# The last weight row and its copy loaded first, each in 16 pieces, and three more filler matmuls ahead of the weight matmuls

## The chip, the cores and the metric

The kernel runs on one core of one Trainium2 chip. The metric is device time in microseconds (us) of one launch; less is better. The engines are named as in the profile: PE is TensorE's matmuls and PEld its weight loads, DVE is VectorE, ACT is ScalarE, POOL is GpSimd, and SP is SyncE, which here does nothing but issue DMAs. An engine name with a q (SPq) is that engine's instruction queue.

## The reference

A circular two-dimensional convolution of one image of 224 x 224 pixels and 96 channels with 7 x 7 weights of 96 x 96, computed with FFTs, in bfloat16 at both ends:

```python
# x: (1, 224, 224, 96)   w: (7, 7, 96, 96)
wp = jnp.pad(w, ((0, H - K), (0, W - K), (0, 0), (0, 0)))
Xf = rfft2(x.astype(float32), axes=(1, 2))
Wf = rfft2(wp.astype(float32), axes=(0, 1))
Yf = einsum('bhwi,hwio->bhwo', Xf, Wf)
y = irfft2(Yf, s=(H, W), axes=(1, 2)).astype(bfloat16)
```

## The kernel before

**How the work is cut.** Along the image's rows the kernel transforms, along its columns it convolves directly. The 224 rows are cut into 8 blocks of 28 rows with 6 rows of overlap, so a block is a signal of length 34, with 17 frequencies of a real and an imaginary part. The 224 columns are cut into 7 tiles of 32 pixels. For each tile, stage A transforms the rows by matmuls of pixels against the matrix `Fm` and puts the result into `xf`; stage B convolves along the columns, frequency by frequency, with the transformed weights `WF` (`b_round`, one call for a frequency), using sums and differences of `xf` that DVE puts into `J`; stage C transforms back by matmuls against `G` and writes the rows out. Between B and C the data passes through a scratch tensor in device memory (`scr`, then `tt`).

**The weights.** The 49 weight matrices (7 x 7 places) are loaded into the tile `wqx`, two partitions for each place k: partition 2k holds the 96 x 96 matrix as one run, and partition 2k + 1 holds the same run shifted by 48 output channels. `PW` is 49, `C` is 96, `C2` is 48, and `WC` is the length of a run, 96 x 96 - 48 = 9168 elements or 18336 bytes. The part of the tile from column `WC` on holds a small matrix `Em`, computed on the chip by DVE, and zeros. One matmul of the loaded weights (the stationary side, with a step of 96 elements from column to column) against `Em` gives the transformed weights of two output channels. `prep_jobs(gi)` makes these matmuls for the frequencies of group gi, four matmuls to a PSUM bank, and `evac` has DVE or ACT copy each bank into `WF`. Every such matmul reads all 98 partitions of `wqx`, so the first one needs every weight DMA to have landed, the last row's too. The page calls the tile wq.

**The order of the DMAs.** All loads of the opening are issued by SP in the program's order (the wrapper `_Ordered` fixes the order of each engine's instructions and of all transfers): first the six wrapped pixels of each half of the block rows (`xh_bufs`), then the 32 pixels of tile 0's first half, `load_x(0, 0)`, then the weights, then tile 0's second half, `load_x(0, 1)`. A pixel load is two DMAs, one of 112 rows and one of 6. The weights are two DMAs as well, one of the first 48 places (96 partitions) and one of the last place (2 partitions):

```python
for k, n in ((0, PW - 1), (PW - 1, 1)):
    dma(wqx[2 * k:2 * (k + n), 0:WC], bass.AP(wsrc.tensor, wsrc.offset + k * C * C, [[C * C, n], [C2, 2], [1, WC]]))
```

The buffers of tile 0's pixels lie in a part of `WF` that is filled late, so the profile shows these loads as WF<-in_x_dram.

**The order of PE's work in the opening.** PE starts with filler matmuls (`warm(n)`: n matmuls of 512 columns on zeros, whose results nobody reads), 17 of them. Stage A of the wrapped pixels and of tile 0's first half follows, then the lines around the second edit:

```python
for _ in range(3):
    warm(9)
for f in prep_jobs(0)[0]:
    f()
last = [f() for f in fj[0][1]]
```

That is 27 fillers, then the 48 matmuls that transform the weights of the first two frequencies (`prep_jobs(0)`), then stage A of tile 0's second half for frequencies 0 to 7 (`fj[0][1]`: 32 matmuls in four banks), whose first copy is also what the loads of tile 1's pixels wait for. After that DVE builds the first `J`, stage B begins with frequency 0, and the other weights are transformed between its matmuls. Which engine copies which bank is fixed when the program is built, by sums of estimated costs; fillers and DMAs add nothing to those sums.

Of the kernel before, what the change touches and what calls it, by code (L numbers as in the profile page):

```python
# [52 lines left out]
def kernel(  # L53
# [7 lines left out]
    _, H, W, C = x.shape  # L61
# [5 lines left out]
    PW = KT * KT  # L67
    FR = 2 * NS
    PW2 = 2 * PW
    C2 = C // 2  # L70
# [37 lines left out]
    def bank():  # L108
        return pools["psb"].tile([128, 512], F32, name="pb")
# [28 lines left out]
    def dma(out_ap, in_ap):  # L138
        return DE.dma_start(out=out_ap, in_=in_ap)
# [20 lines left out]
    wqx = wtmp.tile([128, C - 1 + 127 * C + 1], BF16, name="wq")  # L160
    wq = wqx[0:PW2]
    WC = C * C - C2
# [18 lines left out]
    def load_x(t, jg):  # L181
        return load_rows(xbuf(t, jg), jg, t * 2 * TW, 2 * TW)

    wsrc = w.rearrange("kh kw i o -> (kh kw) (i o)")
    for jg in range(2):
        load_rows(xh_bufs[jg], jg, W - PAD, PAD)
    load_x(0, 0)
    for k, n in ((0, PW - 1), (PW - 1, 1)):
        dma(wqx[2 * k:2 * (k + n), 0:WC], bass.AP(wsrc.tensor, wsrc.offset + k * C * C, [[C * C, n], [C2, 2], [1, WC]]))
    load_x(0, 1)  # L190

    wu = cpool.tile([128, 128], BF16, name="wu")
# [3 lines left out]
    def warm(n):  # L196
        pwu = bank()
        for _ in range(n):
            TE.matmul(pwu[:].rearrange("p (a b) -> p a b", a=4), lhsT=wu[:, 0:128], rhs=wur, start=True, stop=True)
# [489 lines left out]
        for f in fj[p][0]:  # L689
            f()  # L690
    for _ in range(3):
        warm(9)
    for f in prep_jobs(0)[0]:
        f()
    last = [f() for f in fj[0][1]]
# [32 lines left out]
    for gi in range(1, len(PGRP)):  # L728
        pj, dj = prep_jobs(gi)
        add(2 * PGRP[gi - 1][0], 2 * PGRP[gi - 1][1] - 1, pj)  # L730
        for i, f in enumerate(dj):
            k = 2 * (PGRP[gi][0] + i) - 2
# [126 lines left out]
    for i, (g, q) in enumerate(order):  # L859
# [3 lines left out]
        k = i + 8 - LF  # L863
# [37 lines left out]
```

## Time and profile before

| What | Value |
|---|---|
| Median of 4 runs | 277.39 us (275.97 to 277.88) |
| The profiled execution, whole | 277.02 us |
| Its span, first to last instruction | 275.3 us |
| Mean granted TensorE clock | 0.989 |
| PE busy | 261.4 us (95%), 5088 matmuls |
| DVE busy | 227.8 us (83%) |
| ACT busy | 196.5 us (71%) |
| wq matmuls in all | 288, 22.4 us |
| Filler matmuls and the like on `wu` in all | 70, 19.2 us |
| DMA of the 48 places | 1719.0 KB |
| DMA of the last place | 35.8 KB |

The span counts from the first to the last instruction of the profiled execution; its whole time is 1.7 us longer. Nearly every operation passes through the helper on line 87, so the profile's groups are told apart by tiles: pb is a PSUM bank, wu the fillers' zeros, wq the loaded weights, WF the transformed weights (or, early, tile 0's pixels), xf and J the sides of stage B. PE and PEld overlap, and matmuls are pipelined: a single one is shown as about 200 to 380 ns long although the next starts much sooner, so start times tell more than durations. In a view of busy time by stretch, PEclk is the clock that TensorE was granted, 1.00 being the full one.

### The profile page before, as it was taken

To read this page: it belongs to the slowest core of one execution; us is meant where nothing else is said; L and a number is where in the kernel's file an instruction comes from. 1 tells how busy PE (TensorE), PEld (TensorE's weight loads), DVE (VectorE), ACT (ScalarE), POOL (GpSimd) and SP (SyncE) were. 2 spreads that over 40 slices of the span, in tenths; PEclk is the share of its full clock that TensorE was granted. 3 is DMA by queue.
4 is the path that set the end of the run, shared out by engine and by line. 5 is a ranking of instruction groups with operands and counts; after the bars stand their busy time and mean duration, and the time that the engine had idled before them with its cause. 6 is when DMAs were issued, how large, how long until landed. Compare 5 with 4: busy or idle time off the path is not lost.

```text
span 275.3 us, 12056 instructions
## 1 busy us (share of the span) xinstructions
PE 261.4 (95%) x5088; PEld 239.1 (87%) x5088; DVE 227.8 (83%) x469; ACT 196.5 (71%) x475; POOL 101.2 (37%) x152
## 2 busy tenths in 40 slices
PE   8889999989998999999999999999999999999972
PEld 3659998989998999899999999999999989999751
DVE  5528999998999889977976897788988889899932
ACT  5528997768774566898988869888887975553522
POOL 7720033444445453233243215222332242654200
PEclk9997999999999999999999999999999999999998
DMA  7945213411111189887969478877949833989775
GB/s 181 214 118 147 69 48 108 149 46 48 45 69 64 50 251 186 251 230 214 308 197 255 118 227 236 218 193 207 298 144 189 271 125 105 211 217 240 180 193 178
DMA packets 46211, 46.79 MB, mean 170 GB/s; under 512 B 35274, under 2 KB 37846, under 8 KB 46058
## 3 DMA queue, kind: packets, MB, share of 16 engines
q1 hardware_dynamic: 45692, 44.34, 59.1%
q0 software_dynamic: 464, 1.67, 2.0%
q8 instruction: 40, 0.66, 1.1%
q14 instruction: 15, 0.12, 0.2%
HBM read 24.65 MB, written 21.33 MB: 167 GB/s over the span
## 4 chain that ended last, share of the span: by engine, by line
PE 56%; DVE 18%; DMA 10%; issue 7%; POOL 4%; ACT 2%; SPq 2%; DVEq 0%
PE pb L87 56%; DVE J L87 7%; DMA wq<-in_w_dram 5%; DVE v L87 4%; POOL yf L87 4%; DVE WF L87 4%; DMA tt<-scr 3%; DVE u L87 2%; SPq L87 2%; DVE yf L87 1%; DMA xf<-scrl 1%; ACT xf L87 1%; ACT WF L87 1%; DVE yo L87 0%; DVE tt L87 0%
## 5 line engine op out<-in xcount | busy, mean ns | idle before, releaser
L87 PE MATMUL pb<-WF,J 96*128 96x96 bf16 x2898 | 167.5, 206 | 1.4 <-DVE J L87 0.5
L87 PEld LDWEIGHTS <-J 96*128 96x128 bf16 x2898 | 141.5, 98 | 10.7 <-DVE J L87 1.7
L87 POOL TENSOR_TENSOR yf<-v,u 128x384 bf16<-128x384 f32 x85 | 84.2, 1006 | 142.7 <-issue 90.1
L87 ACT CAST xf<-pb 96x408 bf16<-96x408 f32 (+5 forms) x142 | 66.9, 491 | 8.8 <-PE pb L87 6.8
L87 PE MATMUL pb<-WF,xf 96*128 96x96 bf16 x952 | 61.0, 206 | 2.7 <-DVE WF L87 2.2
L87 DVE TENSOR_TENSOR J<-xf 96x1824 bf16<-96x1824 bf16 (+1 forms) x84 | 60.3, 756 | 0.1
L87 PEld LDWEIGHTS <-xf 96*128 96x128 bf16 x952 | 47.4, 98 | 3.6 <-issue 3.1
L87 PE MATMUL pb<-Fm,xn 118*128 118x136 bf16 (+4 forms) x576 | 44.5, 203 | 0.0
L87 ACT CAST WF<-pb 96x480 bf16<-96x480 f32 (+1 forms) x60 | 29.9, 560 | 7.0 <-PE pb L87 6.7
L87 PE MATMUL pb<-tt,Gm 102*84 102x384 bf16 (+1 forms) x132 | 33.6, 326 | 0.0
L87 PEld LDWEIGHTS <-xn 118*128 118x128 bf16 x576 | 29.3, 98 | 0.1
L87 ACT CAST yo<-pb 84x384 bf16<-84x384 f32 (+1 forms) x61 | 26.3, 479 | 4.1 <-PE pb L87 4.0
L87 ACT CAST J<-pb 84x384 bf16<-84x384 f32 (+1 forms) x62 | 26.8, 482 | 2.7 <-PE pb L87 2.6
L87 DVE TENSOR_TENSOR J<-J 96x912 bf16<-96x912 bf16 (+1 forms) x42 | 25.0, 594 | 0.0
L87 PE MATMUL pb<-wq 98*128 98x120 bf16 (+1 forms) x288 | 22.4, 229 | 1.1 <-DMA wq<-in_w_dram 1.1
L87 PEld LDWEIGHTS <-wq 98*128 98x128 bf16 x288 | 20.0, 150 | 1.6 <-issue 1.6
L87 PE MATMUL pb<-wu 128*128 128x512 bf16 (+3 forms) x70 | 19.2, 405 | 1.1 <-DVE ct L87 1.1
L87 DVE TENSOR_TENSOR yf<-v,u 128x384 bf16<-128x384 f32 x27 | 15.6, 578 | 0.9
L87 DVE TENSOR_TENSOR WF<-WF 96x960 bf16<-96x960 bf16 x15 | 15.9, 1057 | 0.2
L87 PEld LDWEIGHTS <-wu 128*128 128x128 bf16 (+3 forms) x70 | 8.0, 117 | 8.8 <-issue 3.5
L87 PEld LDWEIGHTS <-Gm 102*84 102x84 bf16 (+1 forms) x132 | 11.5, 117 | 1.7 <-issue 0.6
L87 DVE CAST WF<-pb 96x400 bf16<-96x400 f32 (+1 forms) x12 | 7.0, 606 | 7.2 <-PE pb L87 7.1
(394 smaller groups left out, 238.6 us busy)
## 6 DMA issues: line engine op xcount, KB each, us to landing
scr<-yf SPq DMA_DIRECT2D x30, 288.0 KB
xn<-in_x_dram SPq DMA_DIRECT2D x12, 672.0 KB
tt<-scr SPq DMA_DIRECT2D x24, 336.0 KB
out_dram<-yo SPq DMA_DIRECT2D x12, 252.0 KB
out_dram<-J SPq DMA_DIRECT2D x12, 252.0 KB
tt<-scr SPq DMA_DIRECT2D x6, 288.0 KB
wq<-in_w_dram SPq DMA_DIRECT2D x1, 1719.0 KB
scrl<-yf POOLq DMA_DIRECT2D x5, 288.0 KB, 5.1
```

The lines of the kernel that those rows point to most:

```text
L87: r = fn(*a, **k)
```

## The change

Where there was one DMA of the first 48 places and then one for the last place's two partitions, there are now three: the last place's row and its shifted copy, one DMA each and each written as 16 runs of 573 elements (1146 bytes) into its one partition, and after them the 48 places. The bytes that land in `wqx` are the same. The three groups of fillers ahead of `prep_jobs(0)` have 10 matmuls instead of 9, so there are 30 instead of 27.

```diff
@@ -185,8 +185,10 @@
     for jg in range(2):
         load_rows(xh_bufs[jg], jg, W - PAD, PAD)
     load_x(0, 0)
-    for k, n in ((0, PW - 1), (PW - 1, 1)):
-        dma(wqx[2 * k:2 * (k + n), 0:WC], bass.AP(wsrc.tensor, wsrc.offset + k * C * C, [[C * C, n], [C2, 2], [1, WC]]))
+    for h in range(2):
+        k = 2 * PW - 2 + h
+        dma(wqx[k:k + 1, 0:WC].rearrange("p (a b) -> p a b", a=16), wsrc[PW - 1:PW, h * C2:h * C2 + WC].rearrange("p (a b) -> p a b", a=16))
+    dma(wqx[0:2 * PW - 2, 0:WC], bass.AP(wsrc.tensor, wsrc.offset, [[C * C, PW - 1], [C2, 2], [1, WC]]))
     load_x(0, 1)
 
     wu = cpool.tile([128, 128], BF16, name="wu")
@@ -689,7 +691,7 @@
         for f in fj[p][0]:
             f()
     for _ in range(3):
-        warm(9)
+        warm(10)
     for f in prep_jobs(0)[0]:
         f()
     last = [f() for f in fj[0][1]]
```

## Prediction

> **What bounds the kernel now.** I read the page's busy shares first: TensorE (PE) is busy for 261.4 of 275.3 us, so a change counts if it moves PE's work. The edit lies in the opening, before 24 us. I therefore read the chain of waits there, from its start to 26 us (columns: start us, us, what):
>
> ```profile
> 3.12 0.71 SPq L87
> 3.87 14.19 DMA wq<-in_w_dram
> 18.06 0.14 issue
> 18.19 4.82 PE pb L87 x72
> 23.01 0.02 issue
> 23.03 0.59 ACT xf L87
> 23.62 0.05 issue
> 23.67 2.34 PE pb L87 x46
> ```
>
> The end is reached through the weights: issued by 3.87, landed at 18.06, and everything after hangs on PE's start at 18.19. Next PE's timeline in order of time (start, us, work, idle before):
>
> ```profile
> 11.07 6.00 PE L87 MATMUL pb<-wu 128*128 128x512 bf16 x27
> 18.19 3.52 PE L87 MATMUL pb<-wq 98*128 98x100 bf16 x48 [1.12 <-DMA wq<-in_w_dram]
> 21.52 1.90 PE L87 MATMUL pb<-Fm,WF 118*128 118x64 bf16 x32
> 23.67 0.51 PE L87 MATMUL pb<-WF,xf 96*128 96x96 bf16 x8 [0.25 <-ACT xf L87]
> 24.02 1.15 PE L87 MATMUL pb<-wq 98*128 98x120 bf16 x16
> ```
>
> The 27 fillers run out at 17.07 and PE idles 1.12 us for wq. The third view is busy time by stretch; I chose stretches along the clock's changes (columns: stretch, length, then PE, PEld, DVE, ACT, POOL busy, PEclk, DMA share, GB/s):
>
> ```profile
> 6.43:9.84 3.41, 2.55 (x43) 1.85 (x42) 2.40 (x5) 1.20 (x3) 2.73 (x15) 1.00 1.00 217
> ...
> 16.67:20.08 3.41, 2.29 (x33) 1.92 (x32) 1.43 (x3) 1.19 (x3) 0.00 (x0) 1.00 0.21 63
> 20.08:23.49 3.41, 3.34 (x52) 3.18 (x50) 2.46 (x6) 2.69 (x6) 0.00 (x0) 0.50 0.00 0
> 23.49:26.91 3.42, 3.24 (x65) 3.25 (x66) 3.31 (x6) 2.99 (x8) 0.36 (x1) 1.00 0.98 259
> ```
>
> After the stretch with the gap, PE gets half its clock for 3.41 us, and then the full one. So the wait costs twice: the gap, and slow matmuls after it.
>
> Fourth, the trace's semaphore increments[...]. The 48-row transfer has 16, from 14.27 to 16.86. The last row and its copy have two: 15.96 and **18.06**. Their packets started behind an engine's own six rows, at 14.68 and 15.65, and took 1.2 us each. The wait is thus for one 18 KB packet on one engine, after the other engines' rows had landed.
>
> [...] 2 increments for the two rows, 6 for six-row loads, 16 for 112 or 96 rows. No run yet shows one partition cut in 16. [...] The packet that started last ended at 16.87, its increment came at 18.06: 1.2 us more[...]. [...] 1.1 us was enough[...]. The 0.83 us gap ahead of 9.11 (2.55 busy in its stretch) had no such effect.
>
> **The change, part by part.** *SP's queue.* Removed: the two-row issue (0.44 us at 3.87). Added: two single-row issues ahead of the 48 rows; I take 0.4 us each, near 0.44 for the two rows and 0.31 to 0.39 for the pixel loads. The 48-row issue moves from 3.12 to 3.9 and ends at 4.65. Pixel load 0 shows 0.64 us from the issue's end (2.70) to its first packet (3.34), so weight packets could start at 5.3. They started at 5.64, when pixel rows freed the engines: hidden, with 0.3 us to spare; without that cover up to 0.8 us late. The second pixel load moves by 0.4 us and sits on the rings behind the weights until 13.5: hidden. SP then has nothing until 22.79. The new issues wait for nothing not already landed (4.02 at the latest).
>
> *The rings.* Each of 16 engines gets two pieces of 1146 B ahead of its six rows. The nearest row is the 1152 B packet of the first pixels, median 51 ns: 0.1 us, with two increments. Bounds: 0 if overlapped with other packets, 0.4 us if crowding doubles it twice. The 48 rows' last landing goes from 16.86 to about 17.0 (16.9 to 17.3); the packet behind it on one engine is gone.
>
> *Fillers.* The 27th starts at 16.69; they follow at 0.216 us, so PE takes the next instruction at 16.91. Three more put that at **17.55**. The weights at 17.0 are 0.5 us earlier, so what is late next is the fillers themselves: 18.19 - 17.55 = **0.64 us** gained. Against 27 fillers with the same landing the three cost about 0.4; they are the price of having no gap.
>
> *The clock.* With no gap the stretch from 16.67 is fully busy and I expect no halved window. Worked forward from 17.55: wq matmuls start every 61 ns at full clock (every 83 after 20.1), 48 x 0.0615 = 2.95, so pixels start at 20.50, not 21.52. But DVE and ACT must empty twelve banks, one each per 0.487 us: their last starts are about 20.72, they are free at 21.20. Four pixel banks follow, ACT and DVE in turn. ACT's two, 0.49 + 0.58, end at 22.28, and the first B-stage matmul, which needs the second, starts at 22.34 rather than 23.67: **1.33 us**. Of that 0.64 is the start and 0.69 the clock (PE alone would save 0.35 on wq and 0.68 on pixels; the evacuations hide part).
>
> *After that.* DVE's second pixel bank ends at 22.48, J's first part takes 1.1 us, to about 23.70. PE reaches the J matmuls 1.74 us after its B-stage start, at 24.08: not late. The second pixel load landed by 19.84, behind the same rows; it is needed at 20.5 now, 0.7 us to spare. Tile 1's pixel loads follow ACT's first pixel copy, so they move with it. From there to 99 us the chain is PE, DVE, ACT and POOL handing on to each other, and the 8.29 us DMA wait at 99.43 follows stores of the same stream: I pass the gain on whole, 0.3 us either way.
>
> *Sum.* The profiled execution took 277.02 us (span 275.3, 1.7 around it): 277.02 - 1.33 = **275.7**. It is 0.37 below the median of 277.39, from which the same sum gives 276.06. [...] I take 275.7 between.
>
> **Rivals.** *A: the start comes earlier, the clock drops all the same,* or the clock's part is given back downstream. For: wq matmuls fill only 0.042 of each 0.061 us, and what counts as activity isn't shown. Against: wq matmuls from 24.02 ran so at full clock. Only 0.64 is left: 276.4 to 276.75.
>
> *B: the weights aren't earlier.* The 16 pieces write one partition, and each row's 18 KB may pass it at one engine's pace (6144 B in 0.234 us at the least, so 0.7 us a row, 1.4 for two). If the late engines stand in that queue, the landing stays at 18.1 to 18.3 with a gap of 0.6 after the fillers, and the clock may be kept. 277.5 to 276.8. Against: engines reach the pieces over two microseconds, not at once.
>
> *C, slower: the pieces don't spread.* The destination's first dimension is one partition; if that decides, 32 pieces run one after another on one engine ahead of its six rows. At 51 ns that is 1.6 us, landing at 18.5 and 277.8. In the crowded stage 6144 B packets took 0.42 rather than 0.23 us; at 100 ns a piece it is 3.2 us, landing 20.1, start 20.2, half clock as before: **279.4**. It is slower by over 0.5% once a piece takes 81 ns ((18.06 - 16.86 + 1.39) / 32). Against: the 48-row transfer's destination shape starts with a 1 and still had 16 increments.
>
> **How the numbers follow.** 0.5% is 1.39 us, about what a measurement of this kernel can tell; faster by more means under 276.0. Likeliest case 0.65: its own range, 275.0 to 276.3 from the two baselines and the 0.3 us, straddles that line; 0.55 of it I put below, 0.10 within. A 0.13 and B 0.09 are within 0.5%, C 0.13 above. So 0.55, 0.32, 0.13. The range reaches from 274.9 to 277.6, leaving out most of C and a little below.
>
> **What would show it.** Right: increments of the small transfers 16 each, before 9 us; the 48 rows' last by 17.3; 30 fillers followed by wq at 17.55 without a gap; PEclk 1.00 from 16 to 27; B stage at about 22.3. Wrong: one engine's increments for a small row (C); wq at 18 or later with a DMA wait (B); a PEclk of 0.50 after 20 (A); B stage early but the span's end not 1.3 us earlier, so a later wait took it.

## The result, and the profile after

The runs show no difference: 276.74 us median (44 runs, 275.26 to 280.33) against 276.95 us for before (63 runs), a ratio of 1.0005 with a 95% interval of 0.9989 to 1.0021. The forecast was 275.7. Every ratio here is the one on record, taken over fast runs alone, and it differs from the quotient of the medians shown by up to 0.2%.

The profiled execution of the change tells another story at first sight. It took 275.77 us, 1.25 less than the profiled one of before, close to the forecast's 1.33. Its chain of waits to 26 us (start us, us, what):

```profile
3.70 14.00 DMA wq<-in_w_dram
17.70 0.05 issue
17.75 0.69 PE pb L87 x8
18.44 0.02 issue
18.46 1.47 ACT WF L87 x3
19.93 0.00 issue
19.93 1.27 ACT WF L87 x3
21.20 1.03 ACT xf L87 x2
22.23 0.05 issue
22.28 2.78 PE pb L87 x54
```

The weights still end the wait, at 17.70 after 18.06, and B still begins early, at 22.28. The timeline of PE (start, us, work, idle before) shows why that isn't the change's doing:

```profile
7.77 2.13 PE L87 MATMUL pb<-Fm,WF 118*128 118x64 bf16 x64 [0.26 <-DMA WF<-in_x_dram]
9.74 6.64 PE L87 MATMUL pb<-wu 128*128 128x512 bf16 x30
17.75 3.13 PE L87 MATMUL pb<-wq 98*128 98x100 bf16 x48 [1.37 <-DMA wq<-in_w_dram]
20.72 1.10 PE L87 MATMUL pb<-Fm,WF 118*128 118x64 bf16 x32
22.28 0.51 PE L87 MATMUL pb<-WF,xf 96*128 96x96 bf16 x8 [0.46 <-ACT xf L87]
```

The first pixels let PE go on at 7.77, not at 9.11, so 30 fillers end before 27 did in the trace of before, and the gap is longer than there: 1.37 us, not 1.12. Busy time by stretch (stretch, length, then PE, PEld, DVE, ACT, POOL busy, PEclk, DMA share, GB/s) shows that the clock stayed whole in spite of it:

```profile
15.18:18.59 3.41, 2.04 (x20) 1.20 (x19) 0.37 (x1) 0.13 (x1) 0.86 (x3) 1.00 0.46 126
18.59:22.00 3.41, 3.23 (x70) 3.11 (x68) 3.24 (x7) 3.41 (x8) 0.00 (x0) 1.00 0.01 4
```

This is a matter of luck. Each run comes with its mean granted clock. A stretch of 3.4 us at half clock (a halved window, from here on) in some 274 us takes 0.006 off that mean. The clock's drop after the last matmul, which costs nothing, takes off nearly as much: 0.0048 in the trace of before (half clock from 272.7 on) and 0.0053 in that of the change (from 271.2 on). I draw the line at 0.9945: in the fourteen traces it parts those with a halved window before the last matmul (eight) from those without (six), and I take it to do so mostly in the runs without a trace. Of the change's 44 runs 22 are below (median 277.49 us), 22 above (275.75). For before, on the chip of the first experiments, it was 40 of 75 (277.22 and 275.23). Both kernels thus fall into two groups of runs whose medians lie 1.7 to 2.0 us apart, and the two traces were two draws.

What the change did to the DMAs stands in the trace's semaphore increments (us):

```
the change: last place's row   8.38
            its shifted copy   9.73
            48 places          14.42 14.53 14.56 ... 15.20 15.53 15.71 17.70
```

The row and its copy have **one increment each**. Their issues in the trace carry one run of 18336 bytes, not 16 of 1146: 16 neighbouring runs in one partition were joined to one again. The trace names no engine for a packet, but the 98 packets of 18 KB fall into 16 chains in which one starts as another ends: fifteen of six packets and one of eight. I take a chain for one of the 16 engines that the page counts. Fifteen of the 16 engines had written out their six rows by 14.69 and posted their increments by 15.71. On the sixteenth two more 18 KB packets ran one behind the other, from 14.18 to 15.43 and from 15.42 to 16.48, and its increment came at 17.70. One engine had both rows ahead of its own six. The new order didn't spread the last rows, it put both on one engine. The added issues delayed nothing: the first 18 KB packet starts at 5.68, against 5.64 before.

### The profile page after: what moved, and what is told of

It reads as the page before. It is cut to its first block, busy times and chain, and to the rows that moved or that the text cites. A ratio compares the mean times of both kernels' runs of the same rounds, so it can differ in the third digit from the quotient of the medians.

```text
span 274.1 us, 12065 instructions
## 1 busy us (share of the span) xinstructions
PE 260.3 (95%) x5091; PEld 238.1 (87%) x5091; DVE 227.6 (83%) x469; ACT 196.1 (72%) x475; POOL 101.3 (37%) x152
## 4 chain that ended last, share of the span: by engine, by line
PE 51%; DVE 20%; DMA 9%; issue 8%; ACT 6%; POOL 3%; SPq 2%; DVEq 0%
PE pb L87 51%; DVE J L87 7%; DMA wq<-in_w_dram 5%; DVE WF L87 4%; DVE v L87 4%; DMA tt<-scr 3%; ACT WF L87 3%; POOL yf L87 3%; DVE u L87 2%; DVE yf L87 2%; SPq L87 2%; ACT xf L87 2%; DMA xf<-scrl 1%; DVE yo L87 0%; DVE xf L87 0%
```

## The experiments

Theories at the start. *One engine*: as just said, the rows aren't spread, so the landing doesn't move. *Clock*: what costs is the halved window after a gap (in the trace of before 3.41 us at 0.50 after 1.12 us), more than the start itself. *Downstream*: an earlier start is absorbed later. Each kernel was timed beside before on one chip. The kernels of the first three parts share one chip and its runs of before; those of the fourth part ("Moving the instruction fetch") and those of the last part have a chip of their own each.

### Each half of the change alone

```diff
 e1_dma_only: the change's DMAs
-        warm(10)
+        warm(9)
 e2_fill_only: before's DMAs
-        warm(9)
+        warm(10)
```

> The new weight DMAs with the old 27 fillers. One-engine theory (each single-row DMA is one 18 KB packet on one engine, ahead of that engine's six rows): 1 increment for each row, the weights still land at 17.5 to 18.1, the gap ahead of the weight matmuls is 1.4 to 2.0 us, time within 0.3% of before. Spreading theory (16 pieces on 16 engines, and the three fillers ate the gain): 16 increments each, weights by 17.3, 0.2 to 0.3% faster than before.

> The old weight DMAs with 30 fillers. Both theories: the weights land as before near 18, the fillers end 0.65 us later, so the gap shrinks to about 0.5 us where the pixels came late and to 1.8 where they came early, and the start does not move. Clock theory (what is slow is not the start but the half-clock window [...]): fewer executions with a half-clock window, 0.1 to 0.3% faster than before. If the gap's clock effect is nothing: 1.000.

The DMAs alone: 276.61 us, ratio **1.0036** (1.0011 to 1.0062), slower; one increment a row, the last of the 48 places' at 17.34, 15 of 22 runs below 0.9945. The fillers alone: 275.24 us, **0.9979** (0.9955 to 1.0002), and 5 of 22 runs below. So the halves pull against each other: the product of the two ratios, 1.0015, lies within the change's interval. The fillers' own interval still takes in no difference, so their gain is likely, not shown. In the trace of the DMAs alone the halved window is there:

```profile
14.80:18.21 3.41, 1.66 (x17) 1.02 (x16) 0.33 (x1) 0.07 (x1) 1.21 (x3) 1.00 0.63 165
18.21:21.62 3.41, 3.41 (x48) 3.41 (x47) 2.69 (x6) 2.77 (x6) 0.00 (x0) 0.50 0.01 5
```

PE was busy for 1.66 of the 3.41 us ahead of it, against 2.04 in the trace of the change, where the clock stayed.

### Rows that are truly spread

```diff
-        dma(wqx[k:k + 1, 0:WC].rearrange(...a=16), wsrc[...].rearrange(...a=16))
+        wd = wqx[k:k + 1, 0:WC].rearrange("p (a b) -> p a b", a=16)
+        ws = wsrc[PW - 1:PW, h * C2:h * C2 + WC].rearrange("p (a b) -> p a b", a=16)
+        for b0, b1 in ((0, 287), (287, 573)):
+            dma(wd[:, :, b0:b1], ws[:, :, b0:b1])
```

Each DMA takes a part of each of the 16 runs, with gaps between, so that no two runs touch.

> As the change, with each of the two rows loaded by two DMAs of 16 runs (287 and 286 elements of each 573), which cannot be joined into one run, so they must spread. One-engine theory: 16 increments for each small DMA, last weight increment by about 17.0, the wait for the weights gone or under 0.3 us, no half-clock window, 0.4 to 0.6% faster than before (275.4 to 275.9 where before is 277). Downstream theory (a later wait absorbs an earlier start): the weights are early all the same but the time stays within 0.1% of before.

275.82 us in the profile, 274.73 us median, **0.9963** (0.9935 to 0.9991): faster, with the increments as expected, 16 for each of the four small DMAs, all by 8.89. The downstream theory falls: what is gained in the opening is gained at the end. (In the profiled executions too: B starts 1.50 us earlier than in the trace of before, and the whole takes 1.20 us less.) But the landing wasn't as expected. Fifteen engines had posted their increments by 16.31, the last did at 17.41, and the gap was still there (the profile puts it down to "issue"; PE started 0.2 us after that last increment):

```profile
9.80 6.64 PE L87 MATMUL pb<-wu 128*128 128x512 bf16 x30
17.61 3.17 PE L87 MATMUL pb<-wq 98*128 98x100 bf16 x48 [1.16 <-issue]
```

No weight packet was under way after 15.44. What was: on the queue that the page calls "q8 instruction" a packet of 16384 bytes from 14.89 to 16.20, and the write of the last increment began at 16.19. The trace of before has 40 such packets too, one for about every 250 of PE's 10176 loads and matmuls, and the page counts only 469, 475 and 152 instructions on DVE, ACT and POOL, so I take them for fetches of PE's instructions. Hence a *fetch* theory: PE's instruction fetch runs on one of the 16 engines and holds back that engine's increment. Before's trace doesn't need it: there the last row's own packet ended only at 16.87, and the increment came 1.2 us later, at 18.06, just as it came here 1.2 us after the write at 16.19.

### No gap

> The change with 36 fillers instead of 30. Fillers end 1.3 us later than with 30, at 17.5 to 18.8, so the weight matmuls start at 18.0 to 18.8, no earlier than before, but without a gap. Clock theory: hardly any execution has a half-clock window, and the time is 0.2 to 0.5% below before in spite of the late start. Start theory (only the start of the weight matmuls counts): 0 to 0.3% slower than before.

The change with `warm(12)`: 275.99 us, 0.9996 (0.9972 to 1.0020), and 1 of 22 runs below 0.9945. In its trace there is no gap:

```profile
9.70 7.94 PE L87 MATMUL pb<-wu 128*128 128x512 bf16 x36
17.47 3.08 PE L87 MATMUL pb<-wq 98*128 98x100 bf16 x48
```

Both the clock theory and the start theory get a part: the draws with the low clock are gone, but the rest sits at 275.98, 0.75 above that of before. The six fillers delay PE where the weights come in time, but in this trace by 0.26 us only (weights there at 17.21), so most of the 0.75 stays unexplained. The expected gain wasn't there.

### Moving the instruction fetch

The 17 first fillers cut into 34 of half the columns:

```diff
-    warm(8)
-    warm(9)
+    warm_half(16)     # 256 columns each
+    warm_half(18)
```

> The truly spread last rows with 30 fillers, and the 17 first fillers cut into 34 of half the columns: the same time on PE, but 34 more instructions, so that PE's instruction fetch of 16 KB, which in all traces so far starts when PE has begun about 242 loads and matmuls (14.6 to 15.1, in the first trace of before 16.4), starts at about 11. Fetch theory (the last increment of the weights is held back by this fetch on the same DMA engine, data packets being over by 15.4): last increment by 16.5, the wait at most 0.3 us, start at 16.3 to 16.7 rather than 17.6, 0.3 to 0.5% faster than the spread kernel without it, so 0.6 to 0.9% faster than before. Receipt theory (the last increment is simply slow by a microsecond on one engine): still 17.2 to 17.5, time as the spread kernel, 0.996 of before.

> Before, with the 17 first fillers cut in halves so that the instruction fetch comes early. Fetch theory: the data of the last row ended at 16.2 in the trace with the old DMAs and 30 fillers, and the last increment comes at 16.3 to 16.7 rather than 17.2; the fillers end near 15.5, the gap shrinks to about 1 us, 0.2 to 0.5% faster than before. Receipt theory: 17.2 and no change.

> The change, with the 17 first fillers cut in halves. Fetch theory: the engine with eight rows ends its data at 16.2 to 16.5 and is now the last alone: last increment 16.4 to 17.2, 0.3 to 0.5 us earlier than in the change, 0.1 to 0.4% faster than before. It should stand behind the spread kernel with the early fetch by 0.2 to 0.5%, which is what the eight rows on one engine cost. Receipt theory: 17.3 to 17.7, no change.

A miss as a test: the fetch did not come earlier, but at 15.33, 14.94 and 15.52. The count of PE's instructions alone didn't set its start here; what did isn't shown. The last increments were 18.05, 17.31 and 17.98. In the first two the write of that increment began as the fetch ended (16.82 against 16.83, 16.23 against 16.25); in the third a weight packet itself ran until 17.01. All three were slower than their unsplit kernels: 1.0012 (0.9984 to 1.0039), 1.0035 (1.0009 to 1.0061) and 1.0053 (1.0032 to 1.0074). The loss is at the other end. The 17 added matmuls and their 17 weight loads shift the later fetches, and the last one, at 264.8 to 266.8 in the six traces before these, moved to 260.6 to 261.9, into the last loads. PE's timeline there, first of the spread kernel, then of its variant:

```profile
264.94 0.99 PE L87 MATMUL pb<-xf,GB 128*112 128x384 bf16 x5 [1.58 <-DMA xf<-scrl]
```

```profile
266.31 0.99 PE L87 MATMUL pb<-xf,GB 128*112 128x384 bf16 x5 [2.37 <-DMA xf<-scrl]
...
268.25 0.52 PE L87 MATMUL pb<-xf,GB 128*112 128x384 bf16 x1
```

The wait for the last planes is 0.8 us longer, and after it the clock is halved (from 267.97 on; these matmuls take 0.52 instead of 0.33 us). All three variants show both: waits of 2.18 to 2.50 us, against 1.44 to 1.70 in all other traces. That the fetch is what lengthens this wait is an inference from its place.

Beside them the change itself ran again:

> The change itself once more, on the chip and beside the runs of before that the others share: 1.000 to 1.003 by all theories, the weights' last increment at 17.2 to 17.7, one increment for each of the two rows; it gives a second trace of the change and the yardstick for the others.

276.23 us, 0.9998 (0.9973 to 1.0024); one increment a row, the last weights at 18.29.

### Without a fetch ahead of the weights

The spread kernel with `warm(1)`, `warm(12)` and `warm(9)`, and before with `warm(12)`:

> The truly spread last rows with 3 fillers instead of 30, one look. With so few instructions PE does not come to its first instruction fetch before it stands at the weights. Fetch theory: no 16 KB instruction packet between 14 and 17 us, the weights' last increment at 16.0 to 16.6, as the other fifteen engines showed; PE idles for some 5 us ahead of the weights, so its clock is halved for at least one window and the time is 276 to 279. Receipt theory: the last increment still comes a microsecond after the others, at 17.2 to 17.6.

This comes nearest to the test that the split fillers failed to be, in one trace. With 3 fillers the first instruction packet starts at 17.81, and **all sixteen** increments of the 48 places are there by 16.38. Of the thirteen traces with a fetch that starts between 14.5 and 16.4, the first trace of before among them, eleven have the last one at 17.2 to 18.3, and two at 16.25 and 16.83. But the eleven have two causes. In four (three with spread rows, one with before's) all weight packets were over by 15.74 and the last write began within 0.02 us of the fetch's end. In the other seven, the two of the change among them, a weight packet itself ended late, at 16.15 to 17.33. PE starts more than a microsecond earlier than with 30 fillers, after an idle time of 5.5 us:

```profile
10.25 0.81 PE L87 MATMUL pb<-wu 128*128 128x512 bf16 x3
16.58 4.18 PE L87 MATMUL pb<-wq 98*128 98x100 bf16 x48 [5.51 <-issue]
20.57 1.60 PE L87 MATMUL pb<-Fm,WF 118*128 118x64 bf16 x32
22.60 0.51 PE L87 MATMUL pb<-WF,xf 96*128 96x96 bf16 x8 [0.44 <-ACT xf L87]
```

It then runs at half clock, 4.18 us for the 48 matmuls where the change took 3.13, and reaches B at 22.60: the clock takes back what the start gave. The single run took 275.60 us, too little to compare.

> The truly spread last rows with 36 fillers. Fillers end at about 17.5, as the last increment comes, so the start is no later than with 30 (17.6) and there is no gap. Clock theory: at most one or two of the executions with a half-clock window in the opening, 0.4 to 0.8% faster than before, and better than with 30 fillers by 0.1 to 0.2%. If only the start counts: as with 30 fillers, 0.996.

> The old weight DMAs with 36 fillers. The fillers end at about 17.5, the weights come at 17.2 or a little later. Clock theory: the gap is what cost, not the order of the rows, so 0.3 to 0.6% faster than before and within 0.2% of the spread kernel with 36. Engine-load theory (the rows on the late engine cost by the start they delay): 0.2 to 0.4% behind the spread kernel with 36.

> The truly spread last rows with the old 27 fillers. It differs from the kernel with the new DMAs and 27 fillers (1.0036) only in that the rows are spread. Engine-load theory: last increment 17.2 to 17.4 rather than 17.3 to 18, 0.2 to 0.4% faster than that kernel: 0.999 to 1.002 of before. Clock theory: the gap grows to 1.7 us, more than half of the executions have a half-clock window, and it is 0.3 to 0.5% slower than with 30 fillers.

| Kernel | Median us | Ratio (95%) | Runs below 0.9945 |
|---|---|---|---|
| spread, 27 fillers | 274.79 | **0.9954** (0.9930 to 0.9978) | 5 of 22 |
| spread, 36 fillers | 275.57 | 0.9990 (0.9970 to 1.0010) | 4 of 22 |
| before's DMAs, 36 fillers | 275.51 | 0.9964 (0.9941 to 0.9986) | 0 of 22 |
| before, the same chip | 276.33 | | 31 of 59 |

Two expectations fail. With spread rows 27 fillers (0.9954) are not seen to be worse than 30 (0.9963, on another chip), and 36 are worse than 27 by 0.78 us in the medians: with 36 PE isn't free before 17.5 even when the weights are there at 16.25, as in the trace of that kernel. (Its four runs below 0.9945 have a median of 275.74, hardly above the others' 275.56, so little was lost in them.) That trace also limits the fetch theory: its fetch ran from 15.07 to 16.49 and held nothing back. The writes of twelve of its sixteen increments had begun by 14.98, so the fetch may have met an engine that was done; which engine a fetch takes the traces don't tell. And before's DMAs do gain from 36 fillers: no run below 0.9945 of 22, and 0.36% with rows that are not spread at all. Its median and that of the spread rows with 36 lie 0.06 us apart, so which of the two is faster stays open.

The cleanest comparison for the rows is that of 27 fillers: joined on one engine 1.0036, as before 1, spread 0.9954 (two chips, each ratio to its own runs of before). The engine with the most rows has eight, seven and six in that order. The packets agree: over all traces the last weight packet ended at 16.15 to 17.33 with the change's DMAs (five traces), at 15.74 to 16.87 with before's (four) and at 15.35 to 15.76 with spread rows (five). The spread version with 27 or 30 fillers is faster than before, and the change is not.

## Why the prediction was wrong

**The rings: the step that failed first.** "Each of 16 engines gets two pieces of 1146 B ahead of its six rows." They got none; one engine got two packets of 18 KB ahead of its six rows. Its last packet ended at 16.48, 1.8 us after those of the other engines, and the last landing was 17.70 (17.2 to 18.3 over the traces of the change's DMAs), not 17.0. The increments followed the access pattern as the instruction carries it: 1 for the joined run, 16 for 16 runs with gaps. That 16 pieces would take 16 engines was my estimate, which no trace of before shows. What I also took for granted was that the 16 runs would reach the instruction. The sign against it was in the diff, runs that touch each other end to end.

**Rival C named this, with the wrong price.** It counted 32 small packets, deciding at 81 ns each. What ran were two of 18 KB; that engine's last two packets took 1.25 and 1.06 us. Since before already had one row too many on an engine, the net is one row more, and the DMAs alone cost 0.36%, about 1.0 us, not the 2.0 us of its 279.4.

**Fillers.** "The 27th starts at 16.69 ... Three more put that at 17.55." That start came from one execution. In the thirteen traces that followed the 64 pixel matmuls start at 7.53 to 8.38; only the first trace of before has 9.11. The thirtieth filler starts at 16.00 in the change, so PE is free near 16.2. With thirty fillers PE waited for the weights in every trace, and my reason for taking the landing as hidden was a late pixel load.

**The landing with spread rows.** Even where the rings step is made true, 17.0 isn't reached every time: 17.41, 17.83 and 18.05 in three traces, 16.25 and 16.38 in two. The instruction fetch was missing from the account of what else is on the rings, although the profile's page lists its queue.

**The clock.** That no gap means few low clocks was right: where the gap is closed they nearly go (36 fillers: 1 of 22 and 0 of 22; with spread rows 4 of 22, hardly slower than the rest). Its size was too small. From the first weight matmul to B it took 4.48 to 4.59 us in the nine traces with the full clock there, and 5.48 to 5.58 in the four with one halved window: 0.9 to 1.1 us, where the forecast had 0.69. The two groups of runs of one kernel lie 1.4 to 2.2 us apart, but that difference also holds whatever makes a gap longer in those runs. And "with no gap" was wrong for the change: its trace has a gap of 1.37 us, and 22 of 44 runs are in the low group.

**Passing on.** That a gain in the opening reaches the end was right: the spread kernels show it. The result is no change, most likely because the DMAs cost (1.0036) about what the fillers gave (0.9979, by itself not clear of noise).

**Smaller readings.** A single-row issue took SP 0.25 us, not 0.4. The gap ahead of 9.11 is 0.86 us, not 0.83. The increment at 15.96 can't belong to the packet that started at 14.68, which ended at 15.91: matched in order of time, the others of that trace follow their packets by 0.75 to 1.2 us. The 1.2 us from a last packet's end to its increment came again, as 1.1 to 1.2 us from write to increment, in the three late ones with spread rows. The 0.042 us that a wq matmul is said to fill is an estimate: 100 columns, at the fillers' 512 in 0.216 us. The forecast rests on none of these.

## What to carry to other kernels

Cutting one partition's run into 16 touching pieces did not spread it here (1 increment), and 16 pieces with gaps did (16): look for the number of increments. Before costing a gap that a filler is to close, look at several executions: one trace can be a late draw, and two traces of two kernels can differ by the forecast amount with no difference between the kernels (here by 1.25 us). Filler matmuls bought clock here and cost start time: with before's DMAs 0 of 22 runs are below 0.9945 with 36 of them, and 31 of 59 with 27, but with spread rows 36 are 0.78 us slower than 27. Their number also moved PE's instruction fetches (with spread rows the first starts at 17.81 with 3 fillers, at 14.89 with 30), and in four traces here a fetch seems to have held back the load that everything waited for.

## What the runs showed of the hardware

- In the opening a gap in TensorE's work of 1.1 to 2.1 us was followed by half its clock (0.50) for 3.41 us in four traces; gaps of 1.0 to 1.4 us were followed by the full clock in six. At the end waits of 2.2 to 2.5 us were followed by half the clock in three traces, and waits of 1.4 to 1.7 us by the full clock in eleven. In the opening, ahead of the halved stretches, PE was busy for 1.3 to 1.8 us of 3.41, and once for 2.29 (before); 2.04 to 2.65 were followed by the full clock. Busy time alone thus doesn't decide, and what does stays open.
- Sixteen touching runs in one partition were carried as one run and gave 1 increment; sixteen runs with gaps gave 16.
- In four traces the write of the last weight increment began within 0.02 us of the end of a 16 KB instruction fetch of 1.3 to 1.5 us, 0.5 to 1.5 us after the last weight packet. With spread rows the increments were then complete at 17.41 to 18.05; in one trace without a fetch at that time they were by 16.38, and in one with a fetch by 16.25.
- An issue of one row took SP 0.25 us, of 16 runs 0.58 to 0.64 us, of 96 rows 0.61 to 0.71 us.
